# A new order for the first batch of a fused attention and mixture-of-experts kernel, with one half's q softmax moved to ScalarE and 24 identity turns on TensorE

## The chip, the cores and the metric

The kernel runs on one core of a Trainium2 chip. The metric is the device time of one execution in microseconds, the median of several runs. A core has a matmul engine (TensorE, "PE" in the profile, with its weight loads as "PEld"), a vector engine (VectorE, "DVE"), an engine for activation functions (ScalarE, "ACT"), a general engine (GpSimd, "POOL"), and queues that issue DMA transfers (here mostly "SP"). Each engine works through its own list of instructions in order. An instruction waits until the semaphores that it names are up, and all that stands behind it on its engine waits too.

## The reference

All data are float32. Three steps follow each other:

```python
# linear attention, 8 batches x 8 heads, 576 tokens, 64 channels
q_s = exp(q - max(q, -1));  q_s /= sum(q_s, -1) + 1e-9       # softmax over the channels
k_s = exp(k - max(k, 2));   k_s /= sum(k_s, 2) + 1e-9        # softmax over the tokens
kv  = einsum('bhsd,bhse->bhde', k_s, v)
x   = einsum('bhsd,bhde->bhse', q_s, kv)   # then laid out as (4608 tokens, 512)

# mixture of 8 experts, top 1: logits = x @ w_gate, e = argmax(logits)
out[token] = gate * sigmoid(x @ w_output_gate)[e] * (relu(x @ w1[e]) @ w2[e])

# second layer
h = max(max(x @ m_w1, x @ m_w2), x @ m_w3);  result = h @ m_wo
```

## The kernel before

Nearly all work is matmuls of the experts and of the second layer, which are run as three products of split operands. Ahead of them stands the attention of one batch and its routing, since the expert's weights to load are known only when the router has chosen. The kernel therefore runs in slots: slot 0 and later issue one group of 12 expert matmuls each (`l1_group`, `l2_group`), and the attention of the following batches, the splitting of weights and the routing are hung between the groups as events. Slots below 0 hold the first batch's attention with no expert work beside it. The list `first` gives its order: entry i becomes the event of slot i - 120. All engines' lists come from this one order, since the schedule is written by hand and nothing is moved afterwards.

A batch is worked in two units of four heads (the second argument 0 or 1), and a unit's result in two pairs (the third argument). The steps of a unit are:

- `load_k`, `load_q`, `load_v`: transfers issued on SP. `load_2` does the three for unit 0 of batch 1.
- `k_max` (DVE, tile `kmx`), `k_tr` (TensorE turns `kmx` into `kT`, DVE reduces it to `m` and makes the diagonal `dg`), `k_exp` (TensorE spreads `dg` as `kB`, DVE subtracts it from `k`, ACT takes the exponential into `ke`).
- `q_max` (DVE, `qm`), `q_exp` (subtraction on DVE, for unit 1 of batch 0 on POOL, then ACT's exponential in place), `q_sum` (DVE sum `qs`, + 1e-9, reciprocal), `q_norm` (DVE, `qn`).
- `kv_mm` (TensorE, 20 small matmuls), `kv_norm` (DVE, `kvraw`, and a transfer to memory).
- per pair: `q_tr` (five TensorE turns of `qn` into the PSUM tile of tag "big", one buffer, copied by ACT to `qTf`), `x_mm` (two matmuls of 288 columns into PSUM tiles of tag "mm", four buffers, which ACT copies to `xr`), the split of `xr` into a high part (ACT, `xs`) and a low part (`x_lo`, DVE, `xs`), and `logit_mm`.
- `logit_tr`, `route_1`, `route_2`: logits to tokens, the choice, counts, and the chosen expert's number, which SP reads to issue the loads of the first weights (`stg`). `route_3` makes the gates.
- `in_2` runs a step for unit 0 of batch 1. That unit's `k_tr` and `k_exp` come in slot 0 and the slots ahead of it (`EARLY`), with the split of the first weights (`w`, high part on ACT, low part on DVE for the first two).

The matmuls of the first expert group (`hp`) stand on TensorE behind that unit's `kB`.

Of the kernel before, what the change touches and what calls it, by code (L numbers as in the profile page):

```python
# [9 lines left out]
F32 = mybir.dt.float32  # L10
# [3 lines left out]
ACTF = mybir.ActivationFunctionType  # L14
ALU = mybir.AluOpType
AX = mybir.AxisListType
# [3 lines left out]
B, H, S, D = 8, 8, 576, 64  # L20
# [8 lines left out]
HF = S // 2  # L29
# [31 lines left out]
def tile_linear_attention__then__moe(  # L61
# [15 lines left out]
    nc = tc.nc  # L77
    dma = nc.sync.dma_start
    gdma = nc.gpsimd.dma_start
    vec = nc.vector  # L80
    act = nc.scalar.activation
    mm = nc.tensor.matmul
# [5 lines left out]
    ident = const.tile([128, 128], F32, name="ident")  # L88
# [35 lines left out]
    ps_mm = es_moe.enter_context(tc.tile_pool(name="ps_mm", bufs=4, space=PSUM))  # L124
# [5 lines left out]
    sm = es_att.enter_context(tc.tile_pool(name="sm", bufs=2, side="right"))  # L130
    dc_p = es_att.enter_context(tc.tile_pool(name="dc_p", bufs=1, side="right"))
    kvz = es_att.enter_context(tc.tile_pool(name="kvz", bufs=1, side="right"))
    ps_at = es_att.enter_context(tc.tile_pool(name="ps_at", bufs=1, space=PSUM, side="right"))
# [49 lines left out]
    units = {}  # L183
# [35 lines left out]
    def k_max(b, hb):  # L219
# [3 lines left out]
            out=u["mx"], in_=u["k"].rearrange("p h c d -> p h d c"), axis=AX.X, op=ALU.max  # L223
        )

    def q_max(b, hb):
        u = units[b, hb]
        qt = u["q"].rearrange("p h c d -> p (h c) d")
        m = sm.tile([128, 20, 1], F32, tag="qm", name="qm")
        vec.tensor_reduce(out=m[:, :, 0], in_=qt, axis=AX.X, op=ALU.max)  # L230
        u["qm"] = m

    def q_exp(b, hb):
        u = units[b, hb]
        qt = u["q"].rearrange("p h c d -> p (h c) d")
        eng = nc.gpsimd if (b, hb) == (0, 1) else vec
        eng.tensor_tensor(out=qt, in0=qt, in1=u["qm"].to_broadcast([128, 20, D]), op=ALU.subtract)
        act(out=qt, in_=qt, func=ACTF.Exp)

    def k_tr(b, hb):  # L240
        u = units[b, hb]
        ps = ps_at.tile([128, 2, 128], F32, tag="kb", name="kT")
        mx = u["mx"].rearrange("p h d -> p (h d)")
        for i in range(2):
            nc.tensor.transpose(ps[:, i], mx[:, 128 * i:128 * i + 128], ident)
        m2 = sm.tile([128, 2], F32, tag="m2", name="m2")
        vec.tensor_reduce(out=m2, in_=ps, axis=AX.X, op=ALU.max)
        u["dg"] = sm.tile([128, 2, 128], F32, tag="dg", name="dg")
        for i in range(2):
            vec.tensor_scalar(  # L250
                out=u["dg"][:, i], in0=ident, scalar1=m2[:, i:i + 1], scalar2=None, op0=ALU.mult
            )
# [93 lines left out]
    def x_mm(b, hb, pr):  # L346
        u = units[b, hb]
        g = 2 * hb + pr
        if b == 0:
            ps = [ps_mm.tile([128, HF], F32, tag="mm", name="xT0") for i in range(2)]  # L350
        else:
            big = ps_at.tile([128, 2, 512], F32, tag="big", name="xT")
            ps = [big[:, i, 0:HF] for i in range(2)]
        qT = u["qT", pr]
        for i in range(2):
            cs = slice(HF * i, HF * i + HF)
            if b < NFULL:
                mm(ps[i], kvraw[hb][:, pr], qT[:, 0, cs], start=True, stop=True)
                continue
            kv = u["kv"]  # L360
            for n, (a, c) in enumerate(((0, 0), (0, 1), (1, 0))):
                mm(ps[i], kv[:, a, pr], qT[:, c, cs], start=(n == 0), stop=(n == 2))
        xr = u["xr", pr] = xr_p.tile([128, S], F32, tag="xr", name="xr")
        if b == 0:
            for i in range(2):
                act(out=xr[:, HF * i:HF * i + HF], in_=ps[i], func=ACTF.Copy)
            if hb == 1:
                return
        else:
            act(out=xr.rearrange("p (a t) -> p a t", a=2), in_=big[:, :, 0:HF], func=ACTF.Copy)  # L370
        t = xp[b, g] = (x_po if b % 2 else x_pe).tile([128, 2, S], F32R, tag="x", name="xs")
        act(out=t[:, 0], in_=xr, func=ACTF.Copy)

    def x_lo(b, hb, pr):
        xr = units[b, hb]["xr", pr]
        if b == 0 and hb == 1:
            t = xp[b, 2 * hb + pr] = (x_po if b % 2 else x_pe).tile([128, 2, S], F32R, tag="x", name="xs")
            act(out=t[:, 0], in_=xr, func=ACTF.Copy)
        t = xp[b, 2 * hb + pr]
        vec.tensor_tensor(out=t[:, 1], in0=xr, in1=t[:, 0].bitcast(F32), op=ALU.subtract)  # L380
# [131 lines left out]
    def in_2(b, f):  # L512
        f(1, 0)

    first = (
        (load_k, 0), (load_k, 1), (load_q, 0), (load_v, 0), (load_q, 1), (load_v, 1),
        (k_max, 0), (k_tr, 0), (k_max, 1), (k_exp, 0), (k_tr, 1), (q_max, 0), (k_exp, 1), (q_exp, 0),
        (kv_mm, 0), (q_max, 1), (q_sum, 0), (kv_mm, 1), (q_norm, 0), (q_exp, 1), (kv_norm, 0), (q_tr, 0, 0), (kv_lo, 0),
        (load_2,), (q_sum, 1), (q_lo, 0, 0), (q_tr, 0, 1), (x_mm, 0, 0), (kv_norm, 1), (q_lo, 0, 1), (kv_lo, 1),
        (q_norm, 1), (q_tr, 1, 0), (x_mm, 0, 1), (logit_mm, 0, 0), (q_tr, 1, 1), (x_mm, 1, 0), (logit_mm, 0, 1),  # L520
        (x_mm, 1, 1), (x_lo, 0, 0), (x_lo, 0, 1), (logit_mm, 1, 0), (logit_mm, 1, 1), (in_2, q_max), (in_2, k_max),
        (logit_tr,), (route_1,), (route_2,), (in_2, q_exp), (x_lo, 1, 0), (x_lo, 1, 1), (route_3,),
    )
    for i, (f, *a) in enumerate(first):
        at(-120 + i, f, 0, *a)
    at(ROUTE0[0], route_4, 0)
    for c in range(5):
        at(ROUTE0[1] + 2 * c, route_5, 0, c)
    START = {n: 16 * n - 51 for n in range(2, 2 * B)}
    FRONT = (q_max, q_exp, k_max, k_tr, k_exp, q_sum, kv_mm, kv_norm, kv_lo, q_norm)  # L530
    BACK = (q_tr, q_lo, x_mm, x_lo, logit_mm)
    for n, s0 in START.items():
        b, hb = divmod(n, 2)
# [345 lines left out]
    with tc.manual_schedule():  # L879
# [55 lines left out]
        def out_ps(nm):  # L935
            return ps_o.tile([128, 512], F32, tag="o", name=nm)
# [401 lines left out]
        for c in range(6):  # L1338
# [41 lines left out]
            for i, (col, x) in enumerate(tiles):  # L1380
                m = CAP if x is None else 128
                if i < 2:
                    ps = o[i]
                else:
                    ps = out_ps("op")
# [16 lines left out]
    with tc.For_i(0, n_trip, 1) as it:  # L1402
# [9 lines left out]
        ps = out_ps("lqT")  # L1412
# [9 lines left out]
        for i in range(4):  # L1422
            ps = out_ps("lm")
# [11 lines left out]
        for f in range(6):  # L1435
# [15 lines left out]
            h = lp.tile([128, 2, SLOT], F32R, tag=f"lh{f}", name="lh")  # L1451
# [3 lines left out]
        ps = out_ps("lo")  # L1455
# [40 lines left out]
```

## Time and profile before

| | us |
|---|---|
| median of 3 runs | 1206.53 |
| lowest, highest | 1205.19, 1210.18 |
| the profiled execution, its own time | 1209.64 |
| its span, first to last instruction | 1207.9 |
| TensorE busy in the span | 1146.5 (95%) |
| VectorE busy | 799.1 (66%) |
| ScalarE busy | 527.4 (44%) |
| GpSimd busy | 411.2 (34%) |

The profiled execution lay 1.69 us outside its span, and 3.11 us above the median of the runs. Busy shares are averages over the whole span; the stretch that the change touches is the first 51 us, and it is read from the order of instructions there.

### The profile page before, as it was taken

How to read it: one execution, taken by the hardware profiler on the slowest of the kernel's cores; microseconds unless marked ns; L12 is line 12 of the kernel's file. 1: busy time of each engine (PE TensorE's matmuls, PEld its weight loads, DVE VectorE, ACT ScalarE, POOL GpSimd, SP SyncE). 2: the span in 40 equal slices, each digit the busy share in tenths (PEclk: the TensorE clock that was granted, in tenths of full speed). 3: DMA queues.
4: the chain of work that ended last, by engine and by line, in shares of the span. 5: the costliest groups of instructions: out<-in, count | busy, mean ns of one | idle time of the engine just before them, and what ended most of it. 6: DMA issues, size and time to landing. Idle time of an engine off the chain costs nothing. (4 is left out here: it accounts for less than half of the span.)

```text
span 1207.9 us, 21422 instructions
## 1 busy us (share of the span) xinstructions
PE 1146.5 (95%) x7626; PEld 1072.1 (89%) x7626; DVE 799.1 (66%) x1500; ACT 527.4 (44%) x1081; POOL 411.2 (34%) x502
## 2 busy tenths in 40 slices
PE   4699999999989999999999999999999999999994
PEld 3599898989989898999999899899899989989983
DVE  7688788787878879655789565555546545564430
ACT  2454454635545453545455433443344244333220
POOL 1156667677666767768342030000000000000000
PEclk9899899999999999999999999999999999999997
DMA  6785557575645764436599588397768848747701
GB/s 162 181 224 135 160 170 218 153 208 156 180 159 170 203 177 137 137 115 204 195 311 311 176 256 285 134 296 242 235 217 272 270 144 286 242 149 221 225 26 41
DMA packets 204207, 234.95 MB, mean 195 GB/s; under 512 B 78253, under 2 KB 122061, under 8 KB 204096
## 3 DMA queue, kind: packets, MB, share of 16 engines
q1 hardware_dynamic: 202384, 233.14, 62.4%
q8 instruction: 62, 1.02, 0.3%
q0 software_dynamic: 1712, 0.39, 0.2%
q14 instruction: 49, 0.40, 0.1%
HBM read 189.56 MB, written 44.13 MB: 193 GB/s over the span
## 5 line engine op out<-in xcount | busy, mean ns | idle before, releaser
L638 PE MATMUL yp<-h,w 128*128 128x288 f32 x1536 | 227.0, 304 | 0.0
L620 PE MATMUL hp<-xs,w 128*128 128x288 f32 x1536 | 218.6, 299 | 0.0
L638 PEld LDWEIGHTS yp<-h,w 128*128 128x128 f32 x1536 | 213.1, 192 | 3.3
L620 PEld LDWEIGHTS hp<-xs,w 128*128 128x128 f32 x1536 | 208.2, 189 | 2.6
L604 POOL TENSOR_TENSOR w<-stg,w 128x512 fp32r<-128x512 f32 x126 | 181.2, 1441 | 68.5 <-ACT w L597 66.7
L1218 PE MATMUL pY<-t,sw 128*128 128x384 f32 (+1 forms) x972 | 193.5, 342 | 1.3 <-ACT s L1227 0.9
L1218 PEld LDWEIGHTS pY<-t,sw 128*128 128x128 f32 x972 | 172.8, 188 | 5.5 <-ACT s L1227 2.1
L1195 POOL DMA_INDIRECT out_dram<-ocx,ftb x1 | 1.0, 981 | 481.7 <-SPq L1402 481.7
L1306 PE MATMUL op<-wo,hc 128*128 128x512 f32 (+1 forms) x666 | 156.2, 394 | 0.0
L1306 PEld LDWEIGHTS op<-wo,hc 128*128 128x128 f32 (+1 forms) x666 | 125.1, 188 | 27.9
L1227 ACT ACTIVATE s<-pY 128x384 f32<-128x384 f32 (+1 forms) x108 | 53.7, 497 | 133.1 <-PE pY L1218 129.2
L626 DVE SCALAR_TENSOR_TENSOR h<-hp,h 128x288 fp32r<-128x288 f32 x128 | 56.6, 451 | 54.8 <-ACT h L625 54.4
L625 ACT ACTIVATE h<-hp 128x288 fp32r<-128x288 f32 x128 | 52.3, 409 | 83.1 <-PE hp L620 82.6
L597 ACT ACTIVATE w<-stg 128x512 fp32r<-128x512 f32 x128 | 78.9, 620 | 0.0
L1218 PE MATMUL pY<-B,sw 128*128 128x384 f32 (+1 forms) x324 | 66.4, 340 | 0.5 <-DVE y L645 0.5
L1218 PE MATMUL pZ<-B,sw 128*128 128x384 f32 (+1 forms) x324 | 66.8, 341 | 0.1
L1218 PE MATMUL pX<-B,sw 128*128 128x384 f32 (+1 forms) x324 | 66.9, 341 | 0.0
L1218 PE MATMUL pX<-t,sw 128*128 128x384 f32 (+1 forms) x324 | 66.5, 340 | 0.0
L1234 ACT ACTIVATE hc<-c 128x384 fp32r<-128x384 f32 (+1 forms) x72 | 38.2, 531 | 61.4 <-DVE c L1257 61.1
L1218 PEld LDWEIGHTS pZ<-B,sw 128*128 128x128 f32 x324 | 58.0, 188 | 2.2 <-DVE c L1251 0.4
L1218 PEld LDWEIGHTS pX<-B,sw 128*128 128x128 f32 x324 | 57.7, 188 | 1.7
L1218 PEld LDWEIGHTS pY<-B,sw 128*128 128x128 f32 x324 | 57.7, 188 | 1.7 <-DVE y L645 0.8
(246 smaller groups left out, 1764.0 us busy)
## 6 DMA issues: line engine op xcount, KB each, us to landing
sw<-ws_d SPq DMA_DIRECT2D x315, 256.0 KB, 3.5
stg<-in_moe_w_dram SPq DMA_DIRECT2D x31, 1024.0 KB, 5.3
ws_d<-sw SPq DMA_DIRECT2D x63, 256.0 KB, 3.4
fw<-in_moe_w_dram SPq DMA_DIRECT2D x48, 256.0 KB, 4.1
v<-in_v_dram SPq DMA_DIRECT2D x80, 128.0 KB, 4.7
draw<-in_moe_w_dram SPq DMA_DIRECT2D x24, 384.0 KB, 4.0
k<-in_k_dram SPq DMA_DIRECT2D x16, 512.0 KB, 5.3
q<-in_q_dram SPq DMA_DIRECT2D x16, 512.0 KB, 6.9
```

The source lines that it names most:

```text
L597: act(out=t[:, 0], in_=src, func=ACTF.Copy)
L604: eng.tensor_tensor(out=t[:, 1], in0=src, in1=t[:, 0].bitcast(F32), op=ALU.subtract)
L620: mm(ps, w[:, a, kk], xp[b, kk][:, c, cs], start=(n == 0), stop=(n == 11))
L625: act(out=h[:, 0, cs], in_=ps, func=ACTF.Relu)
L626: vec.scalar_tensor_tensor(out=h[:, 1, cs], in0=ps, scalar=0.0, in1=h[:, 0, cs].bitcast(F32), op0=ALU.max, op1=ALU.subtract,)
L638: mm(ps, w[:, a, f], ht[f][:, c, cs], start=(n == 0), stop=(n == 11))
L1195: nc.gpsimd.indirect_dma_start(out=out[:, :], out_offset=bass.IndirectOffsetOnAxis(ap=tb[0:n, 0:1], axis=0), in_=src, in_offset=None, boun ...
L1218: mm(ps[:, 0:nn], w[:, a, kap], tt_[key, kap][:, cc, 0:nn], start=(start and k == 0), stop=(k == 5), skip_group_check=True)
L1227: act(out=t[:, 0:n_of(c)], in_=pst[n, "X" if nm == "sx" else "Y"][:, 0:n_of(c)], func=ACTF.Copy)
L1234: act(out=h[:, 0, cols], in_=t[:, 0:nn], func=ACTF.Copy)
L1306: mm(ps[0:m], hc[f][:, a, col:col + m], wo[f][:, cc], start=(f == F_ORDER[0] and i == 0), stop=(f == F_ORDER[5] and i == 2))
```

## The change

It touches the first batch only, and within it:

- Unit 0's q. `q_neg` takes the negated maximum on DVE. `q_rows` then issues 20 small ACT instructions of 128x64, one for each (head, chunk), which take exp(q - max) with the maximum as a bias of each partition and give the row's sum in the same instruction (5 of them ahead of unit 0's `ke`, 15 behind it). DVE's subtraction and its sum over `q` for unit 0 are gone; `q_inv` keeps the + 1e-9 and the reciprocal.
- `spin` issues 24 turns of the identity into the PSUM tile "big". Nothing reads the result.
- Unit 1's `kT` goes to a PSUM tile of tag "mm" in place of "kb".
- Of unit 1, the second half of each `xr` is copied by DVE in place of ACT. The high part of `xs` for unit 0 is now made in `x_lo`, as it was for unit 1.
- The list `first` has another order; the diff has it whole.

```diff
+    def q_neg(b, hb):
+        u = units[b, hb]
+        qt = u["q"].rearrange("p h c d -> p (h c) d")
+        m = u["qm"] = sm.tile([128, 20, 1], F32, tag="qm", name="qm")
+        vec.tensor_reduce(out=m[:, :, 0], in_=qt, axis=AX.X, op=ALU.max, negate=True)
+        u["qs"] = sm.tile([128, 20, 1], F32, tag="qs", name="qs")
+
+    def q_rows(b, hb, i0, i1):
+        u = units[b, hb]
+        qt = u["q"].rearrange("p h c d -> p (h c) d")
+        for i in range(i0, i1):
+            act(out=qt[:, i], in_=qt[:, i], func=ACTF.Exp, bias=u["qm"][:, i], accum_out=u["qs"][:, i])
+
+    def q_inv(b, hb):
+        s = units[b, hb]["qs"]
+        vec.tensor_scalar(out=s, in0=s, scalar1=1e-9, scalar2=None, op0=ALU.add)
+        vec.reciprocal(out=s, in_=s)
+
+    def spin(b, n):
+        ps = ps_at.tile([128, 1024], F32, tag="big", name="spin")
+        for i in range(n):
+            nc.tensor.transpose(ps[:, 0:128], ident, ident)
...
-    def q_exp(b, hb):
+    def q_exp(b, hb, parts=(0, 1)):
...
+        if 0 in parts:
+            eng.tensor_tensor(out=qt, in0=qt, in1=u["qm"].to_broadcast([128, 20, D]), op=ALU.subtract)
+        if 1 in parts:
+            act(out=qt, in_=qt, func=ACTF.Exp)
...
+        if (b, hb) == (0, 1):
+            ps = ps_mm.tile([128, HF], F32, tag="mm", name="kT0")[:, 0:256].rearrange("p (i d) -> p i d", i=2)
+        else:
+            ps = ps_at.tile([128, 2, 128], F32, tag="kb", name="kT")
...
         if b == 0:
             for i in range(2):
-                act(out=xr[:, HF * i:HF * i + HF], in_=ps[i], func=ACTF.Copy)
-            if hb == 1:
-                return
+                if i == 1 and hb == 1:
+                    vec.tensor_copy(xr[:, HF:S], ps[1])
+                else:
+                    act(out=xr[:, HF * i:HF * i + HF], in_=ps[i], func=ACTF.Copy)
+            return
...
-        if b == 0 and hb == 1:
+        if b == 0:
...
     first = (
         (load_k, 0), (load_k, 1), (load_q, 0), (load_v, 0), (load_q, 1), (load_v, 1),
-        (k_max, 0), (k_tr, 0), (k_max, 1), (k_exp, 0), (k_tr, 1), (q_max, 0), (k_exp, 1), (q_exp, 0),
-        (kv_mm, 0), (q_max, 1), (q_sum, 0), (kv_mm, 1), (q_norm, 0), (q_exp, 1), (kv_norm, 0), (q_tr, 0, 0), (kv_lo, 0),
-        (load_2,), (q_sum, 1), (q_lo, 0, 0), (q_tr, 0, 1), (x_mm, 0, 0), (kv_norm, 1), (q_lo, 0, 1), (kv_lo, 1),
-        (q_norm, 1), (q_tr, 1, 0), (x_mm, 0, 1), (logit_mm, 0, 0), (q_tr, 1, 1), (x_mm, 1, 0), (logit_mm, 0, 1),
-        (x_mm, 1, 1), (x_lo, 0, 0), (x_lo, 0, 1), (logit_mm, 1, 0), (logit_mm, 1, 1), (in_2, q_max), (in_2, k_max),
-        (logit_tr,), (route_1,), (route_2,), (in_2, q_exp), (x_lo, 1, 0), (x_lo, 1, 1), (route_3,),
+        (k_max, 0), (k_tr, 0), (q_neg, 0), (q_rows, 0, 0, 5), (k_exp, 0), (q_rows, 0, 5, 20), (k_max, 1),
+        (k_tr, 1), (q_max, 1), (q_exp, 1, (0,)), (k_exp, 1), (kv_mm, 0), (spin, 24), (q_inv, 0), (q_norm, 0), (q_tr, 0, 0),
+        (q_exp, 1, (1,)), (kv_norm, 0), (kv_mm, 1), (q_tr, 0, 1), (load_2,), (q_sum, 1), (x_mm, 0, 0), (q_norm, 1),
+        (x_mm, 0, 1), (kv_norm, 1), (logit_mm, 0, 0), (q_tr, 1, 0), (logit_mm, 0, 1), (in_2, q_max),
+        (x_lo, 0, 0), (q_tr, 1, 1), (x_mm, 1, 0), (x_lo, 0, 1), (x_mm, 1, 1), (logit_mm, 1, 0), (logit_mm, 1, 1),
+        (logit_tr,), (route_1,), (route_2,), (in_2, k_max), (in_2, q_exp), (x_lo, 1, 0), (x_lo, 1, 1), (route_3,),
     )
```

On TensorE, from unit 1's turn of `kmx` to the first product of `x`, the kernel before has (`kv_305` is unit 0's small product, `kv_332` unit 1's; line numbers are those of each kernel's file):

```order
L245 MATMUL kT<-ident,kmx 128x128 x2
L257 MATMUL kB<-dg,ones 128x256
L295 MATMUL kv_305<-v_199,ke 64x65 x20
L295 MATMUL kv_332<-v_200,ke 64x65 x20
L329 MATMUL qT<-ident,qn 128x128 x4
L330 MATMUL qT<-ident,qn 128x64
L329 MATMUL qT<-ident,qn 128x128 x4
L330 MATMUL qT<-ident,qn 128x64
L358 MATMUL xT_394<-qTf,kvraw_202 128x288
```

and the changed kernel, from the same turn (`kv_327` is unit 0's, `kv_392` unit 1's):

```order
L275 MATMUL kT_311<-ident,kmx 128x128 x2
L287 MATMUL kB<-dg,ones 128x256
L325 MATMUL kv_327<-v_199,ke 64x65 x20
L249 MATMUL spin<-ident 128x128 x24
L359 MATMUL qT<-ident,qn 128x128 x4
L360 MATMUL qT<-ident,qn 128x64
L325 MATMUL kv_392<-v_200,ke 64x65 x20
L359 MATMUL qT<-ident,qn 128x128 x4
L360 MATMUL qT<-ident,qn 128x64
L388 MATMUL xT_436<-qTf,kvraw_202 128x288
```

The 24 identity turns stand where unit 1's product stood, and that product has moved behind the first pair's turns.

On VectorE, behind the choice of the expert (`mi` is its number, `nm` the last row of `route_2`; `k`, `q`, `kmx` and `qm` are now those of batch 1), the kernel before has:

```order
L437 TENSOR_SCALAR mi<-mc 128x1
L441 COPY cs<-cnt 128x80
L443 TENSOR_SCALAR nm<-v_502,mc 128x8
L237 TENSOR_TENSOR q<-q,qm 128x1280
L380 TENSOR_TENSOR xs<-xr,xs 128x576 x2
L453 TENSOR_TENSOR rz<-roh,rl 128x40
```

and the changed kernel:

```order
L469 TENSOR_SCALAR mi<-mc 128x1
L473 COPY cs<-cnt 128x80
L475 TENSOR_SCALAR nm<-v_542,mc 128x8
L222 TENSOR_REDUCE kmx<-k 128x256
L263 TENSOR_TENSOR q<-q,qm 128x1280
L412 TENSOR_TENSOR xs<-xr,xs 128x576 x2
L485 TENSOR_TENSOR rz<-roh,rl 128x40
```

The maximum over batch 1's `k`, which stood ahead of the logits' turn, now stands between the routing and the subtraction.

## Rows read from the trace of the kernel before

**Rows 1.** Windows: busy us and instructions of each engine, granted clock, DMA
```profile
core 0: us, PE busy (x) PEld busy (x) DVE busy (x) ACT busy (x) POOL busy (x), PEclk, DMA share, GB/s
0.00:51.21 51.21, 24.97 (x176) 16.57 (x177) 36.67 (x77) 18.02 (x29) 5.99 (x22) 0.93 0.64 151
51.21:1207.90 1156.69, 1121.53 (x7452) 1055.58 (x7450) 762.44 (x1423) 509.41 (x1052) 405.19 (x480) 0.98 0.63 196
```

**Rows 2.** Timeline of TensorE: start, us, operation, count [idle before <-releaser]
```profile
15.07 1.19 PE L257 MATMUL kB<-dg,ones 128*128 128x256 f32 x2 [1.12 <-DVE dg L250]
16.20 6.02 PE L295 MATMUL kv<-v,ke 128*64 128x65 f32 x80
24.93 1.12 PE L329 MATMUL qT<-ident,qn 128*128 128x128 f32 x4 [2.71 <-DVE qn L277]
...
31.81 2.11 PE L358 MATMUL xT<-qTf,kvraw 128*128 128x288 f32 x4
...
34.29 0.66 PE L329 MATMUL qT<-ident,qn 128*128 128x128 f32 x4
...
35.09 1.24 PE L358 MATMUL xT<-qTf,kvraw 128*128 128x288 f32 x4
...
37.87 0.98 PE L390 MATMUL lgT<-xr,wgt 128*32 128x128 f32 x20
...
50.58 1.19 PE L257 MATMUL kB<-dg,ones 128*128 128x256 f32 x2 [8.03 <-DVE dg L250]
51.21 3.25 PE L620 MATMUL hp<-xs,w 128*128 128x288 f32 x12
54.66 1.83 PE L295 MATMUL kv<-v,ke 128*64 128x65 f32 x40 [0.20 <-ACT ke L262]
```

**Rows 3.** Waits of TensorE from 51.2 us on: total us, times, longest
```profile
PE xT L362 <- DVE qTs L344: 14.3, 6, 2.6
```

**Rows 4.** Windows around slow stretches of TensorE, columns as in the first group
```profile
50.60:54.10 3.50, 3.50 (x13) 3.32 (x14) 2.72 (x4) 0.77 (x1) 0.00 (x0) 0.50 1.00 351
...
123.70:126.40 2.70, 0.06 (x2) 0.03 (x1) 2.70 (x4) 1.08 (x1) 1.85 (x3) 0.88 0.55 185
126.40:132.60 6.20, 6.20 (x24) 5.95 (x25) 3.76 (x7) 3.84 (x6) 3.87 (x4) 0.50 0.41 110
```

**Rows 5.** Timeline of VectorE, same columns
```profile
9.50 2.32 DVE L222 TENSOR_REDUCE kmx<-k 128x256 f32<-128x1280 f32 x1
...
22.05 0.99 DVE L269 TENSOR_SCALAR qs<-qs 128x20 f32<-128x20 f32 x1
...
23.39 1.49 DVE L277 TENSOR_TENSOR qn<-q,qs 128x1280 f32<-128x1280 f32 x1
...
37.18 2.37 DVE L222 TENSOR_REDUCE kmx<-k 128x256 f32<-128x1280 f32 x1
...
43.58 1.49 DVE L237 TENSOR_TENSOR q<-q,qm 128x1280 f32<-128x1280 f32 x1
46.97 1.43 DVE L380 TENSOR_TENSOR xs<-xr,xs 128x576 fp32r<-128x576 f32 x2 [1.91 <-ACT xs L378]
...
49.95 0.48 DVE L250 TENSOR_SCALAR dg<-ident,m 128x128 f32<-128x128 f32 x2
```

**Rows 6.** Timeline of ScalarE and of GpSimd, same columns
```profile
45.10 1.27 ACT L238 ACTIVATE q<-q 128x1280 f32<-128x1280 f32 x1 [4.84 <-DVE q L237]
...
20.68 2.33 POOL L237 TENSOR_TENSOR q<-q,qm 128x1280 f32<-128x1280 f32 x1 [15.88 <-DVE qm L230]
```

**Rows 7.** Unit 0's q, second transfer: its issue, then size and us to landing
```profile
3.51 1.23 SPq L196 DMA_DIRECT2D q<-in_q_dram  x1
...
q<-in_q_dram SPq DMA_DIRECT2D x1, 128.0 KB, 6.9
```

**Rows 8.** Groups of ScalarE instructions: count | busy us, mean ns | idle before
```profile
L1329 ACT ACTIVATE oc<-op,tsrc 128x512 f32<-128x512 f32 x32 | 22.0, 689 | 59.1 <-PE op L1306 45.7 <-issue 13.4
L1129 ACT ACTIVATE fraw<-fm 128x512 f32<-128x512 f32 x9 | 5.4, 598 | 4.7 <-PE fm L1108 4.7
L394 ACT ACTIVATE lgt<-lgT 32x64 f32<-32x64 f32 x8 | 1.6, 197 | 0.0
```

More of the change, by code (lines that the diff above doesn't have):

```diff
@@ L236, in q_exp @@
         eng = nc.gpsimd if (b, hb) == (0, 1) else vec
-        eng.tensor_tensor(out=qt, in0=qt, in1=u["qm"].to_broadcast([128, 20, D]), op=ALU.subtract)
-        act(out=qt, in_=qt, func=ACTF.Exp)
+        if 0 in parts:
+            eng.tensor_tensor(out=qt, in0=qt, in1=u["qm"].to_broadcast([128, 20, D]), op=ALU.subtract)
+        if 1 in parts:
+            act(out=qt, in_=qt, func=ACTF.Exp)
     def k_tr(b, hb):
         u = units[b, hb]
-        ps = ps_at.tile([128, 2, 128], F32, tag="kb", name="kT")
+        if (b, hb) == (0, 1):
+            ps = ps_mm.tile([128, HF], F32, tag="mm", name="kT0")[:, 0:256].rearrange("p (i d) -> p i d", i=2)
+        else:
+            ps = ps_at.tile([128, 2, 128], F32, tag="kb", name="kT")
         mx = u["mx"].rearrange("p h d -> p (h d)")
```

## Prediction

> **What bounds the kernel now.** I read the windows first. From 51.21 us to the end TensorE is busy 1121.5 of 1156.7 us; ahead of it, 25.0 of 51.2 [rows 1]. So the end is set by TensorE, by a stream that starts with the first expert group `hp` at 51.21 [rows 2], and its largest waits later (six, 14.3 us in all) are for VectorE inside the stream [rows 3]. What happens ahead of `hp` counts one to one: whatever moves its start moves the end. The sum is thus the start of `hp`.
>
> Second, TensorE's timeline, for what it waits for and at which clock. The clock column is no help ahead of the first change of level: it reads full speed from the start, yet `kB` takes 1.19 us at 15.07, the same as at 50.58, where the window shows 0.50 [rows 2, 4]. So until about 33 us the engine runs at the lower level, 1.2 GHz. At 24.93 four turns take 1.12 us and the pair of `x` at 31.81 takes 2.11; at 34.29 and 35.09 the same work takes 0.66 and 1.24, at 2.4 GHz [rows 2]. Unit 0's and unit 1's small products, 6.02 us without a break from 16.20, did not raise it; the mix of turns and `x` products around 31.81 did.
>
> Third, VectorE's timeline behind the choice of the expert: the subtraction at 43.58, ACT's exponential at 45.10, ACT's high parts, VectorE's low parts at 46.97 after 1.91 us of waiting for them, the gates, `dg` at 49.95, `kB` at 50.58, `hp` at 51.21 [rows 2, 5, 6]. This is a chain from 43.58 to 51.21, 7.6 us, in which each step waits for the one before.
>
> **The change part by part.**
>
> *To unit 0's small product.* Before, `kmx` of unit 1 started at 9.50, as soon as VectorE was free [rows 5]. Now `q_neg` stands there. It needs unit 0's q, whose second transfer was issued at 3.51 and took 6.9 us: 10.4 [rows 7]. VectorE idles 0.9 us, takes the maximum (1.5 by the row of the same 1280 elements, `qn` [rows 5]) to 11.9, subtracts from k (1.5) to 13.4, and starts unit 1's `kmx` (2.3) only there. So `kmx` ends at 15.65 in place of 11.82. From there to `kB` it was 3.25 us, of which the subtraction, now ahead, was 1.4: `kB` at 17.5 in place of 15.07 [rows 2], +2.4. Unit 0's product stands behind it on TensorE's list: 18.7 to 21.7 (half of 6.02 [rows 2]) in place of 16.2 to 19.2.
>
> *The rows on ACT.* Twenty instructions of 64 elements with a pointer as bias and a sum. Not in the trace. Below: the 64-element copy, 0.197 us. For the pointer: 0.689 against 0.598 us for 512 elements with and without one, +0.09 [rows 8]. That is 0.29. The sum's price shows in no row; I bound it by nothing and by as much again, so 0.2 (they overlap and the sum is free) to 0.6, and take 0.3, nearest to the rows. ACT starts at 11.9, does five (1.5), `ke` of unit 0 (1.3), fifteen (4.5): done at 19.2, at 0.6 at 25. The Trainium skill (ScalarE: Activation LUTs, What ACT_TABLE_LOAD costs) gives 280 ns plus 0.833 ns an element with a pointer and an overlap of 93 ns back to back, from which I estimate 0.24 us a row and an end at 18; no price of the sum is there.
>
> *q ready.* VectorE takes unit 1's q maximum (17.4 to 18.9), then its subtraction from k to 20.4. GpSimd's subtraction starts with that maximum, 18.95 to 21.3 (2.33 [rows 6]). Before, the + 1e-9 took 0.99 us at 22.05 and ended just when GpSimd did, at 23.01 to 23.04 [rows 5, 6]; the same stall now ends at 21.3. Reciprocal, `qn` (1.49): ready at 23.2, against 24.88 [rows 5]. The removed subtraction and sum (3 us) thus give 1.7, since the later `kmx` takes the rest.
>
> *The identity turns.* They start at 21.7 behind unit 0's product. Four turns start within 0.65 us at the low clock and 0.33 at the high one: by 1.12 and 0.66 less a last turn of some 0.45 and 0.3 [rows 2], about 0.215 and 0.11 each. 24 of them are 5.2 us low, 2.6 high. All low, they end at 26.9; high at once, at 24.3. Both are behind `qn` at 23.2, so the turns, not q, set the first `q_tr`. This is the cover of the rows on ACT too: up to about 0.5 us a row they cost nothing. The turns would raise the clock at some point if they count as the mix ahead of 33 us did, which held turns. I take a rise near the end of the spin: `q_tr` at 26.8 in place of 24.93, **+1.9**.
>
> *From there to the last logit.* Before: 24.93 to 38.85, 13.9 us, nearly 9 of it at the low clock. Now at the high one: four `q_tr` at 0.8 (34.29 to 35.09), unit 1's small product that came in here (1.83), four pairs of `x` at 1.24, four `lgT` at 0.49 [rows 2]: 3.2 + 1.8 + 5.0 + 2.0 = 12.0. Unit 1's exponential now stands on ACT behind the copy of the first `qT`, so its sum, reciprocal and `qn` end some 6.4 us after the first `q_tr`, just as TensorE has done the 6.4 us that stand ahead of unit 1's first turns: perhaps 0.5 of waits. 12.5 against 13.9, **-1.4**. The copies moved from ACT to VectorE and the later high parts lie beside this.
>
> *`k_max` of batch 1.* Before, its 2.37 us at 37.18 lay under the wait for the logits: free. Now it stands at the head of the 7.6 us chain, ahead of the subtraction, and nothing in that chain waits for anything but itself: **+2.4**. Loading the first weights starts from `mi`, ahead of it, and is done within the chain, so it covers nothing.
>
> Sum: 1.9 - 1.4 + 2.4 = **+2.9**: `hp` at about 54.1, the profiled execution at 1209.64 + 2.9 = 1212.5. That execution was 3.1 above the median of the runs, 1206.53, so for a median 1206.53 + 2.9 = **1209.4**.
>
> **The rivals.**
>
> *The turns don't raise the clock* (slower). The small products are short matmuls with a weight load each, as the turns are, and 6.02 us of them raised nothing [rows 2]. Then the spin ends at 26.9, unit 1's product takes 3.0, the turns some 1.4 a pair, and `x` starts at 32.5; the clock rises some 5 us into `x`, as before, at 36 to 39. The stretch takes 15.5 to 17.3 in place of 13.9. +2.0 + 1.6 to 3.4 + 2.4 = +6.0 to +7.8: 1212.5 to 1214.3. It decides if the first `q_tr` still runs low, that is if 24 turns count no more than the small products did. The Trainium skill (TensorE: Matmul & The Clock Gate, Part 4: PE-mode transpose) speaks for it: turns do not count as a busy engine the way matmuls do. The trace agrees only in part: turns were part of the work ahead of the rise near 33 us.
>
> *The later drops of the clock fall otherwise* (faster). In each batch TensorE waits some 2.4 us for VectorE; around the first such wait the clock fell, and the 6.2 us behind it ran at 0.50 [rows 4]. Half of 6.2 is 3.1 us for that one; a drop half as long would cost half of that, and there are six of the waits [rows 3]. Another start of the stream against the clock's own rhythm can lose two to four of these drops, or gain: 1209.4 - 4 to - 7, 1202 to 1205.5. For it: runs of the kernel before differ by 5 us. Against: the waits stay as long as they were.
>
> *The rows on ACT are dear.* At 0.8 us each, a third above my upper bound, q is ready at 31.3, the spin has long ended, and all that follows the first `q_tr` is 4.5 us later than forecast: 1214. Little speaks for it.
>
> **How the numbers follow.** Forecast (1207.5 to 1211.5) 0.55, turns without effect 0.24, drops otherwise or clock up early 0.17, dear rows 0.04. The range takes in most of the second and third: 1204.5 to 1214. Half a per cent, about what a measurement of this kernel tells from no change, is 6 us. Slower by more (above 1212.6) is most of the second and fourth case: 0.20. Faster by more (below 1200.5) needs nearly all drops gone: 0.04. Within: 0.76.
>
> **What would show it.** Right: `hp` at 53.5 to 55 in TensorE's timeline, `qT` starting right behind the last spin near 26.5 with turns at 0.11 us, `kmx` of batch 1 between `nm` and the subtraction, and the idle ahead of `kB` grown by over 2 us. Wrong: four turns of `qT` at 1.12 us behind the spin (the clock stayed down); `qT` waiting for `qn` after the spin (rows dearer than 0.5 us); `hp` ahead of 51.2, in which case the chain behind the routing wasn't the bound that I take it for.

## The result, and the profile after

The changed kernel is slower: 1217.99 us (median of 10 runs, 1213.72 to 1220.86) against 1210.04 for the kernel before beside it (10 runs, 1205.19 to 1211.91), ratio 1.0065 [1.0052, 1.0079]. Run once more beside other kernels it gave 1.0047 [1.0031, 1.0062]. The forecast was 1209.4 and "no change". Its profiled execution took 1213.72 us, span 1212.0.

Windows of the kernel after, split at its first `hp`; busy us and instructions of each engine, then granted clock, DMA share, GB/s; they answer [rows 1]:

```profile
0.00:53.02 53.02, 24.71 (x200) 17.99 (x201) 34.79 (x77) 22.21 (x66) 5.98 (x22) 0.89 0.64 161
53.02:1212.00 1158.98, 1120.27 (x7452) 1053.83 (x7450) 765.92 (x1423) 508.52 (x1052) 407.92 (x480) 0.98 0.62 195
```

`hp` starts 1.81 us later than before. But the stretch behind it, with the same 7452 matmuls, also takes 2.3 us longer (1158.98 for 1156.69), with TensorE busy 1.3 us less: it waits more. The profiled execution is the quickest of its ten runs; at the median there are some 4 us more, which one profile can't place.

TensorE's timeline after: start, us, operation, count [idle before and what ended it]; it answers [rows 2]:

```profile
17.65 1.19 PE L287 MATMUL kB<-dg,ones 128*128 128x256 f32 x2 [1.12 <-DVE dg L280]
18.77 3.02 PE L325 MATMUL kv<-v,ke 128*64 128x65 f32 x40
21.72 4.09 PE L249 MATMUL spin<-ident 128*128 128x128 f32 x24
25.87 0.66 PE L359 MATMUL qT<-ident,qn 128*128 128x128 f32 x4
...
37.83 0.52 PE L422 MATMUL lgT<-xr,wgt 128*32 128x128 f32 x10 [0.46 <-ACT xr L399]
...
45.60 0.69 PE L275 MATMUL kT<-ident,kmx 128*128 128x128 f32 x2 [3.64 <-DVE kmx L222]
52.39 1.19 PE L287 MATMUL kB<-dg,ones 128*128 128x256 f32 x2 [6.10 <-DVE dg L280]
53.02 3.44 PE L652 MATMUL hp<-xs,w 128*128 128x288 f32 x12
```

The turns run 21.72 to 25.8, and the four turns of `qT` right behind them take 0.66 us, not the 1.12 of [rows 2]: the clock is up. From there to the end of the last `lgT` it is 12.48 us. The waits ahead of `kT` and `kB` of batch 1 are those of the late `k_max`.

ScalarE's, VectorE's and GpSimd's timelines after, same columns; they answer [rows 5, 6]:

```profile
12.51 0.33 ACT L238 ACTIVATE q<-q,qm 128x64 f32<-128x64 f32 x1
12.74 0.19 ACT L238 ACTIVATION_READ_ACCUMULATOR q<-q,qm 128x1 f32 x1
12.84 0.33 ACT L238 ACTIVATE q<-q,qm 128x64 f32<-128x64 f32 x1
...
10.64 1.49 DVE L231 TENSOR_REDUCE qm<-q 128x20 f32<-128x1280 f32 x1 [1.10 <-DMA q<-in_q_dram]
...
20.28 1.06 DVE L242 TENSOR_SCALAR qs<-qs 128x20 f32<-128x20 f32 x1
...
18.98 2.33 POOL L263 TENSOR_TENSOR q<-q,qm 128x1280 f32<-128x1280 f32 x1 [14.19 <-DVE qm L255]
```

A row on ScalarE is two instructions, the second reading out the sum. The second starts 0.23 us behind the first, and the next row 0.10 behind that, so row follows row at 0.33 us (12.51 to 12.84).

TensorE's waits: us, times, longest. First those of the kernel after, over the whole execution (8.4 us of `kB` lie ahead of `hp`), then, from 60 us on, those of the kernel before with 24 turns added (e5 below):

```profile
PE xT L392 <- DVE qTs L374: 14.3, 6, 2.6
PE kB L287 <- DVE dg L280: 11.9, 8, 6.1
PE pY L1250 <- ACT s L1259: 2.5, 2, 1.6
...
PE hp L652 <- DVE h L658: 0.5, 1, 0.5
```
```profile
PE xT L367 <- DVE qTs L349: 14.2, 6, 2.6
PE kB L262 <- DVE dg L255: 3.6, 6, 1.0
PE hp L625 <- DVE h L631: 2.0, 1, 2.0
```

`xT` for `qTs` is as in [rows 3]. A wait of `hp` for `h`, near 577 us, is new: the profile of the kernel before has none.

### The profile page after: what moved, and what is told of

The parts are those of the page before. It is cut to its first block, busy times and chain, and to the rows that moved or that the text cites. A ratio compares the mean times of both kernels' runs of the same rounds, so it can differ in the third digit from the quotient of the medians.

```text
span 1212.0 us, 21511 instructions
## 1 busy us (share of the span) xinstructions
PE 1145.0 (94%) x7650; PEld 1071.8 (88%) x7650; DVE 800.7 (66%) x1500; ACT 530.7 (44%) x1118; POOL 413.9 (34%) x502
## 5 line engine op out<-in xcount | busy, mean ns | idle before, releaser
L657 ACT ACTIVATE h<-hp 128x288 fp32r<-128x288 f32 x128 | 52.2, 408 | 82.5 <-PE hp L652 82.1
```

What stands on the lines that cost most here:

```text
L657: act(out=h[:, 0, cs], in_=ps, func=ACTF.Relu)
```

## Experiments

Each ratio is to the kernel before, run on the same chip beside it. "Stretch" is the span less the start of the first `hp`, in one profiled execution. That start varies from execution to execution by up to about 1 us, and the executions of one kernel lie up to 9 us apart, so one stretch settles little; the ratios decide.

| run | ratio | first `hp` | stretch |
|---|---|---|---|
| kernel before | 1 | 51.21 | 1156.7 |
| e1 changed kernel again | 1.0047 [1.0031, 1.0062] | 53.32 | 1159.4 |
| e2 without the turns | 1.0018 [1.0000, 1.0036] | 54.01 | 1156.0 |
| e12 without the turns, again | 1.0027 [1.0014, 1.0039] | 54.26 | 1157.1 |
| e3 with `k_max` early | 1.0054 [1.0038, 1.0070] | 53.89 | 1161.3 |
| e8 with 12 turns | 1.0036 [1.0023, 1.0048] | 52.22 | 1158.5 |
| e6 with the turns late | 1.0052 [1.0034, 1.0070] | 53.20 | 1162.8 |
| e9 six long matmuls for the turns | 1.0075 [1.0056, 1.0095] | 56.98 | 1159.0 |
| e10 24 one-column matmuls for the turns | 1.0041 [1.0023, 1.0060] | 54.35 | 1160.8 |
| e11 96 of them | 1.0085 [1.0065, 1.0106] | 57.18 | 1160.9 |
| e17 turns, padded to 256 instructions | 1.0027 [1.0014, 1.0041] | 54.60 | 1162.4 |
| e4 before, `k_max` late | 1.0009 [0.9994, 1.0025] | 53.46 | 1156.0 |
| e5 before, 24 turns | 1.0028 [1.0013, 1.0044] | 51.19 | 1161.9 |
| e7 before, 36 turns late | 1.0028 [1.0014, 1.0041] | 50.97 | 1163.5 |
| e13 before, 24 one-column at the start | 1.0034 [1.0022, 1.0047] | 50.49 | 1163.8 |
| e14 before, 64 one-column at the start | 1.0007 [0.9996, 1.0018] | 50.02 | 1158.9 |
| e15 before, 20 turns at the start | 1.0050 [1.0036, 1.0063] | 50.27 | 1162.6 |
| e16 before, 24 one-column at the end | 1.0010 [1.0000, 1.0021] | 50.86 | 1159.2 |
| e18 before, 24 turns, padded to 256 | 0.9996 [0.9982, 1.0011] | 50.58 | 1159.7 |

### Which part costs (e1 to e4)

e1 is the changed kernel, unaltered.

> The changed kernel once more, unaltered, since its profiled execution (1213.72 us) was the fastest of ten runs around 1218. Theory A: the typical run is one in which the 24 identity turns do not raise the clock in time; a profile near 1218 then shows four turns of qT at 1.12 us behind the spin and hp starting at 56 to 58 us. Theory B: the spin raises the clock in every run, hp starts near 53 us, and the missing 4 us are lost later, at the low clock behind hp or in the batches.

e2 takes the turns out:

```diff
-(kv_mm, 0), (spin, 24), (q_inv, 0),
+(kv_mm, 0), (q_inv, 0),
```

> The changed kernel without the 24 identity turns; nothing that is computed is left out. Theory A (the turns usually run low and raise nothing): the first qT starts near 23.3 us in place of 25.9 to 26.9, the rest runs low as before, hp starts at 54 to 55.5 and the time is 2 to 4 us below the changed kernel. Theory B (the turns raise the clock): hp starts 1 to 2 us later than the 53.0 of the changed kernel's profile, and the time is 1 to 2 us above it.

e3 moves `k_max` of batch 1 back ahead of the last logits:

```diff
-(in_2, q_max), ... (route_2,), (in_2, k_max), (in_2, q_exp),
+(in_2, q_max), (in_2, k_max), ... (route_2,), (in_2, q_exp),
```

> The changed kernel with batch 1's k_max put back ahead of the logits' turn, behind q_max; nothing else. Theory A and B alike: the 7.7 us chain from the routing to hp loses 2.3 us, but on VectorE the 2.3 us now push the copies of xr that the last logits wait for by some 1.5 us, so that hp starts 0.8 us earlier, at about 52.2. If the whole 2.3 us are saved (hp at 50.7), the copies had slack that I don't see; if none, the move was free.

e4 does the opposite to the kernel before:

```diff
-(in_2, q_max), (in_2, k_max), (logit_tr,), (route_1,), (route_2,), (in_2, q_exp),
+(in_2, q_max), (logit_tr,), (route_1,), (route_2,), (in_2, k_max), (in_2, q_exp),
```

> The kernel before with one part of the change alone: batch 1's k_max moved behind route_2. If the 2.4 us of k_max stand on the chain to hp one to one, hp starts at 53.4 to 53.6 in place of 51.2 and the time is 2 to 2.5 us above the kernel before. If the chain has slack, under 1 us.

In e1 the four turns of `qT` behind the spin take 0.66 us again and `hp` starts at 53.32: the turns do raise the clock, and the loss lies behind `hp` (theory B). Without turns the first `hp` is later than with them (54.0 to 54.3 for 53.0 to 53.3), yet the kernel is quicker by 0.0020 to 0.0047, 2.4 to 5.7 us (e1 and e2, run beside each other, took 1216.29 and 1212.60). So neither theory of e2 holds whole: the turns help ahead of `hp`, by about 1 us, and lose more than 3 us behind it. e4 shows the price of the late `k_max`: 2.25 us at `hp`, and some 1 us at the end, where the interval takes in anything from nothing to 3. e3 shows that in the changed order the early place isn't free either: `hp` at 53.89, not at the 52.2 expected. TensorE's timeline of e3:

```profile
38.82 0.52 PE L422 MATMUL lgT<-xr,wgt 128*32 128x128 f32 x10 [1.33 <-ACT xr L399]
40.68 0.52 PE L422 MATMUL lgT<-xr,wgt 128*32 128x128 f32 x10 [1.35 <-ACT xr L399]
```

The last two logits now wait 1.3 us each, in the changed kernel 0 and 0.46. VectorE's and ScalarE's timelines of e3 show why:

```profile
35.23 2.37 DVE L222 TENSOR_REDUCE kmx<-k 128x256 f32<-128x1280 f32 x1
37.50 0.76 DVE L412 TENSOR_TENSOR xs<-xr,xs 128x576 fp32r<-128x576 f32 x1
...
38.35 0.41 ACT L399 ACTIVATE xr<-xT 128x288 f32<-128x288 f32 x1 [2.32 <-DVE xs L412]
```

VectorE's low part of unit 0's `x` (37.50) now stands behind `kmx`, and ScalarE's copy of unit 1's `x` needs the buffer that it reads.

### Do the turns cost by the start of hp, by their number, by their place? (e5 to e8)

e5 and e7 add turns to the kernel before; e6 and e8 alter those of the changed kernel:

```diff
 # e5, kernel before: behind unit 1's small product
-(kv_mm, 1), (q_norm, 0),
+(kv_mm, 1), (spin, 24), (q_norm, 0),
 # e6, changed kernel: from their place to the wait between routing and kB
-(kv_mm, 0), (spin, 24), (q_inv, 0), ... (x_lo, 1, 1), (route_3,),
+(kv_mm, 0), (q_inv, 0), ... (x_lo, 1, 1), (route_3,), (spin, 24),
 # e7, kernel before: in that wait
-(x_lo, 1, 1), (route_3,),
+(x_lo, 1, 1), (route_3,), (spin, 36),
 # e8, changed kernel
-(spin, 24)
+(spin, 12)
```

> The kernel before with one part of the change alone: the 24 identity turns behind both small products, in TensorE's 2.7 us of idle time there. The turns end near 26.5 us, so the first qT starts 1.6 us later, but all up to the logits runs at the high clock: hp between 50.3 and 51.5. Theory N (the turns cost only what they shift hp by): the time stays within 1 us of the kernel before. Theory S (runs with the turns lose some 3 us more to waits behind hp, as three profiles with them against three without suggest): 2.5 to 4 us above the kernel before.

> The changed kernel with the same 24 identity turns moved to TensorE's idle time between the routing and batch 1's kB, so that the number of instructions is the same as in the changed kernel. hp starts as without the turns, near 54.0. Theory N: the time is that of the kernel without turns (1212.6) or up to 2 us less, if the turns keep the clock up for hp (12 matmuls in 1.9 us in place of 3.3). Theory S in the form that the extra instructions themselves cost, wherever they are: near 1216 to 1217. Theory S in the form that the place counts: near 1212.

> The kernel before with 36 identity turns in the idle time between the routing and batch 1's kB, to bring hp up at the high clock. At the low clock they take 7.7 us of an idle time of 8, at the high one 4. If they raise the clock, hp starts at 51.2 as before, but its first 12 matmuls take 1.9 in place of 3.25 us and the time falls by 1 to 2 us. If the clock at hp's start is not worth that in the end, the time is that of the kernel before.

> The changed kernel with 12 identity turns in place of 24. They end at 24.3 in place of 25.9 to 26.4 us, still behind qn (23.1). If the clock has risen by then or rises in the small product behind them, hp starts 1 to 2 us earlier than with 24, at 51.5 to 52.5, and the time falls by as much, to about 1215.5; if it doesn't rise before the x products, hp starts at 54 to 55 and the time is near the 1212.6 of the kernel without turns only if the later loss goes with the early clock, else near 1217 to 1218.

e5 is the telling one. Its `hp` starts at 51.19, as in the kernel before, and expert group 240 at 569.78 against 569.73; it then loses 3.8 us at one place (the 1.3 more in the second layer are within what that layer takes from profile to profile, 611.9 to 616.9 us). TensorE's timeline there, first of the kernel before, then of e5:

```profile
569.73 12.88 PE L620 MATMUL hp<-xs,w 128*128 128x288 f32 x96
582.45 12.88 PE L638 MATMUL yp<-h,w 128*128 128x288 f32 x96
```
```profile
557.06 12.88 PE L643 MATMUL yp<-h,w 128*128 128x288 f32 x96
569.78 6.51 PE L625 MATMUL hp<-xs,w 128*128 128x288 f32 x48
578.31 8.15 PE L625 MATMUL hp<-xs,w 128*128 128x288 f32 x48 [2.01 <-DVE h L631]
```

Turns in the late wait (e6, e7) lose as much, and the gain that e7 was to bring did not come. e8's 12 turns raised the clock too (`hp` at 52.22) and lose as much behind `hp`. So neither the start of `hp` nor the time that the turns take explains the loss; it goes with their being there. The order of the instructions on the other four engines is the same, row for row, with the turns and without them.

### Number, or time and clock? (e9 to e12)

e9 to e11 replace the body of `spin` in the changed kernel; e12 is e2 again.

```diff
-nc.tensor.transpose(ps[:, 0:128], ident, ident)                # x24
+nc.tensor.matmul(ps[:, 0:512], lhsT=ident, rhs=<ident, 4 times>)  # e9, x6
+nc.tensor.matmul(ps[0:1, 0:1], lhsT=ident[:, 0:1], rhs=ident[:, 0:1])  # e10 x24, e11 x96
```

> The changed kernel, with the 24 identity turns replaced by 6 plain matmuls of the identity with four copies of itself (128x512): about the same TensorE time (24 x 0.17 us = 4.1 us) from a quarter of the instructions. Theory A (the loss behind the first expert matmul goes with the number of extra TensorE instructions): near the kernel without turns, ratio 1.0010 to 1.0030, stretch behind the first expert matmul 1156 to 1157.5 us. Theory B (it goes with TensorE's work and the raised clock ahead of that matmul): like the changed kernel, 1.0040 to 1.0065, stretch 1159 us or more. Under both the clock rises before the first q transpose (near 24 us).

> The changed kernel, with each of the 24 turns replaced by a matmul of one column by one column: the same number of instructions, hardly any TensorE work, so the clock should rise only near 33 us as it did without turns. Theory A (number of instructions): like the changed kernel, ratio 1.0040 to 1.0065, stretch behind the first expert matmul 1159 us or more. Theory B (TensorE's work and clock): like the kernel without turns, 1.0010 to 1.0030 and 1156 to 1157.5 us.

> As the run before with 96 one-column matmuls, the dose for theory A. Theory A: more than the 24 turns cost, ratio 1.007 or more (four times the 0.0035 between the kernel with and without turns would be 1.016). Theory B: up to the TensorE time that they take (96 matmuls of some 0.03 to 0.06 us, 3 to 6 us, in an idle time of 4.5 us): 1.0010 to 1.0045.

> The changed kernel without the turns once more, on the chip of the three runs beside it. If the turns carry the loss: ratio 1.0005 to 1.0030, stretch behind the first expert matmul near 1156 us. If the first reading of it was luck of the build or of the runs: 1.0040 or more.

e9 tells number and time not apart: each plain matmul was run in two passes, so that the six took 7.65 us, not 4.1, and held up the first `qT` until 29.61; it lost 9.1 us with `hp` 5.8 us late. A one-column matmul takes two passes as well, so e10 added 96 instructions and not the 48 of the turns. It ran low until 33 us, as without turns, and its ratio is higher than that of e12 beside it (1.0041 for 1.0027), but the intervals overlap: it speaks against theory B without settling it. e11's ratio lies where theory A has it, but 2.8 us of it are a later `hp` (the 96 filled 5.13 us). Behind `hp` its profile lost no more than e10's (1160.9 for 1160.8), and its ratio some 2.5 us more, for four times the instructions: little for a price per instruction. The next runs settle both.

### Extra instructions that cost no time (e13 to e16)

The kernel before, with one-column matmuls or turns ahead of everything, where TensorE waits until 7.94 us; in e16 behind its last output matmul.

```diff
-(k_max, 0), (k_tr, 0),
+(spin, 24), (k_max, 0), (k_tr, 0),     # e13, e14: one-column, 24 and 64; e15: 20 turns
```

> The kernel before, with 24 one-column matmuls (96 TensorE instructions, some 1.3 us) at the very start, where TensorE waits until 7.94 us anyway; the first expert matmul should stay near 51.2 us. Theory A (the shift of TensorE's instructions behind them costs): ratio 1.0020 to 1.0040, stretch behind the first expert matmul 1159 us or more. Theory B (the loss needs TensorE's time or clock in the prologue's last 30 us): 0.9985 to 1.0015, stretch near 1157 us.

> As the run before with 64 of them (256 instructions, some 3.4 us, still inside TensorE's first idle time). Theory A: loss again, 1.0020 to 1.0040; were it to vanish while 24 lose, it would go with the place in a block of code and not with the number. Theory B: 0.9985 to 1.0015.

> The kernel before, with 20 identity turns (40 instructions, 5 to 6 us at 0.27 us each) at the very start, in the same idle time; if they raise the clock there, the first rise is recorded well ahead of 33 us and the prologue may gain up to 2 us. Theory A: 1.0010 to 1.0040. Theory B: the clock falls back in the waits that follow, so 0.9970 to 1.0015.

> The kernel before, with the 24 one-column matmuls behind TensorE's last output matmul, where only the program's size changes and nothing stands behind them. Theory A (shift of what is behind) and theory B: 0.9985 to 1.0020. If the program's size or layout alone costs: 1.0020 to 1.0040.

TensorE's timeline of e13:

```profile
1.44 1.34 PE L229 MATMUL spin<-ident 128*1 128x1 f32 x48 [1.44 <-POOL ident masks.py:199]
7.91 0.69 PE L250 MATMUL kT<-ident,kmx 128*128 128x128 f32 x2 [5.14 <-DVE kmx L222]
```

24 matmuls of one column (96 instructions, two passes with a weight load each) are done 5 us before anything waits for TensorE, `hp` starts 0.7 us earlier than before, and the kernel loses 1.0034. With 256 instructions (e14) it loses nothing that can be told, 1.0007, and the two intervals don't overlap. At the end of the program (e16) 96 cost at most little, 1.0010. So extra instructions lose without any work or clock near `hp` (theory B falls), but not by their number (theory A's dose falls too): what matters is where the instructions behind them come to stand, and 256 brings that back. e15's 40 lose no less than the 96.

What repeats every 256? The queues' rows on the pages of the kernel before and the changed one (packets, MB, share of 16 engines):

```profile
q8 instruction: 62, 1.02, 0.3%
```
```profile
q8 instruction: 63, 1.03, 0.3%
```

In the records each q8 packet has 16,384 bytes, and one comes about every 128 matmuls with their 128 weight loads. I read it as TensorE's code, 64 bytes an instruction. Extra instructions move all later packets in the work. Counted from the start of expert group 224 (of 256, twelve matmuls each), the packets around it come at -10.7, +5.0 and +24.7 us in the kernel before and at -10.9, +5.2, +25.0 with 256 more (e14); with 48 more at -15.2, +2.2, +19.2 (the changed kernel) and -14.2, +2.4, +19.2 (e5); with 96 more at -18.3, -1.3, +16.5 (e13).

### Padding to 256 (e17, e18)

The changed kernel, and e5, each with 52 one-column matmuls (208 instructions) at the very start, to make 256 with the 48 of the turns:

```diff
-(k_max, 0), (k_tr, 0),
+(pad, 52), (k_max, 0), (k_tr, 0),     # pad: one-column matmuls, as in e10
```

> The changed kernel, turns and all, with 52 one-column matmuls (208 instructions, some 2.9 us) at the very start, where TensorE waits until 7.9 us; with the turns' 48 that makes 256 instructions more than without both. Theory F (the place of the 16,384-byte instruction transfers in the work decides): the transfers come back to where the kernels without extra instructions have them (near -11, +5 and +25 us from the start of the expert group number 224; the changed kernel has -15, +2 and +19), stretch behind the first expert matmul 1155.5 to 1157.5 us, hp near 53.2 as in the changed kernel, so ratio 1.0005 to 1.0030. Theory A (any extra TensorE instruction costs): 1.0045 to 1.0070.

> The kernel before with the 24 turns behind unit 1's kv products (e5: ratio 1.0028, stretch 1161.9 us) and the same 208 instructions at the very start. Theory F: the loss goes, ratio 0.9985 to 1.0015, stretch near 1157 us, no wait of hp for h near 577 us (2.0 us in e5). Theory A: 1.0025 to 1.0045 and the wait stays.

Both ratios came as theory F has them and below what theory A has. The q8 packets stand at -10.6, +5.1, +26.4 (e17) and -10.8, +4.8, +25.5 (e18). e18 against e5: 0.9996 for 1.0028, intervals apart. e17 against the changed kernel: 1.0027 for 1.0065 (apart) and 1.0047 (they overlap); it equals the kernel without turns (1.0018, 1.0027). e17's and e18's stretches missed (1162.4 and 1159.7, expected up to 1157.5): e17's profiled execution, 1218.75, was the longest of its twelve, 3.5 above their median. Its `hp` missed too, 54.60 for 53.2: unit 1's turn of `kmx` already started 0.9 us later than in e1 (16.75 for 15.84), and the turns took 4.95 us. TensorE's timeline of e18 at the place where e5 waited 2.01 us:

```profile
571.01 13.06 PE L630 MATMUL hp<-xs,w 128*128 128x288 f32 x96
583.91 12.88 PE L648 MATMUL yp<-h,w 128*128 128x288 f32 x96
```

No wait. What may carry it from the code's packets to TensorE shows in SP's queue. Between 562 and 566 us in e5, the row of q8 (packets, MB, share), and SP's timeline, which is the issue of transfers:

```profile
q8 instruction: 1, 0.02, 1.7%
```
```profile
562.95 0.47 SPq L761 DMA_DIRECT2D srb<-w_d  x1
563.46 1.61 SPq L762 DMA_DIRECT2D srb<-w_d  x1
565.11 0.47 SPq L761 DMA_DIRECT2D srb<-w_d  x1
```

and in e18, where no q8 packet falls there:

```profile
563.73 0.48 SPq L767 DMA_DIRECT2D srb<-w_d  x1
564.25 0.47 SPq L766 DMA_DIRECT2D srb<-w_d  x1
564.76 0.47 SPq L767 DMA_DIRECT2D srb<-w_d  x1
```

The issue that coincides with the packet takes 1.61 us instead of 0.47; the changed kernel has one of 1.46 at 564.47, with its packet. Over all twenty profiles, of SP's issues between 55 and 600 us that overlap a q8 packet 41 to 65% took over 0.9 us, of the others 11 to 14%. A long issue overlaps something more easily, but that is not it: by the packets that were under way 0.235 us behind an issue's start it is 38 to 71% against 11 to 15%. Behind it everything that SP still has to issue comes 1 us later, and the work on it slides along. In e5 VectorE's splits of the second layer's operands then fall beside GpSimd's work. VectorE's timeline of the kernel before, then VectorE's and GpSimd's of e5:

```profile
572.58 1.02 DVE L875 TENSOR_TENSOR B<-yr,B 128x384 fp32r<-128x384 f32 x2
573.52 1.85 DVE L782 TENSOR_TENSOR sw<-s,sw 128x256 fp32r<-128x256 f32 x2
575.30 0.45 DVE L626 SCALAR_TENSOR_TENSOR h<-hp,h 128x288 fp32r<-128x288 f32 x1
```
```profile
572.92 3.23 DVE L880 TENSOR_TENSOR B<-yr,B 128x384 fp32r<-128x384 f32 x2
576.06 1.82 DVE L787 TENSOR_TENSOR sw<-s,sw 128x256 fp32r<-128x256 f32 x2
577.81 0.45 DVE L631 SCALAR_TENSOR_TENSOR h<-hp,h 128x288 fp32r<-128x288 f32 x1
...
571.11 4.62 POOL L609 TENSOR_TENSOR w<-stg,w 128x512 fp32r<-128x512 f32 x3
```

The two `B` take 3.23 us (1.02 in the kernel before, 2.00 in e18), while GpSimd runs three splits of the first layer's weights from 571.11 to 575.7; `h` comes at 577.81 (575.30), and TensorE waits for it.

This wait sorts the twenty profiles. Eight kernels have TensorE's code where it stood or 256 further on (the kernel before, e2, e4, e12, e14, e16, e17, e18): seven have no wait of `hp` for `h` there, e12 has one of 0.7 us. Of the twelve others eleven have it, with 0.3 to 2.4 us, and only e10 has none. The times say the same: the loss by the ratio, less what the first `hp` came later, is -1.2 to +2.0 us in the seven of the eight that have a ratio, and 1.8 (e10) to 7.0 us in the twelve. In single profiles the two overlap more: from the first `hp` to the end of the experts 541.2 to 546.7 us against 544.1 to 549.1.

**Shown** is that the place of TensorE's code within blocks of 256 instructions decides some 2.4 to 4.6 us, as measured by adding and taking away instructions that do nothing. That the packets act by holding up SP's issues is **read from the trace, not tested alone**, and I have not followed each of the other waits (`kB`, the second layer's `pY` and `pZ`) to one packet. Why e15's 40 instructions lose as much as e13's 96 is open too.

No version beats the kernel before: e18, the quickest, is level with it.

## Why the prediction was wrong

By its own steps:

- **To unit 0's small product**: right. `kB` 17.65 (forecast 17.5), the product 18.77 to 21.8 (18.7 to 21.7).
- **The rows on ACT**: right. 0.33 us a row, within 0.2 to 0.6 and near the 0.3 taken; the last starts at 19.63. The sum is an instruction of its own, 0.19 us, of which 0.10 lengthen the step from row to row and the rest lies beside the next row. The Trainium skill (ScalarE: Activation LUTs, What ACT_TABLE_LOAD costs) gives 280 ns plus 0.833 ns an element with a pointer and an overlap of 93 ns, from which I estimated 0.24 us; the trace agrees, since a row takes 0.33 us and its sum starts 0.23 behind it, and what was missing is the sum's 0.10.
- **q ready**: right. `qn` 21.69 to 23.2 (23.2), the stall on + 1e-9 ends at 21.3 with GpSimd. Without turns `qT` starts at 23.85 (e12), so the turns do set the first `qT`, as said.
- **The turns**: mechanism right, size a little off. They raise the clock, though sooner than taken: 4.09 us in place of 5.1, `qT` at 25.87 in place of 26.8, so +0.9 and not +1.9 (4.58 us and 26.37 in e1). The first rival, that they don't raise it, fell: 24 turns, and nothing else, stand between the small product at 1.2 GHz and `qT` at 2.4. What spoke for it in the Trainium skill (TensorE: Matmul & The Clock Gate, Part 4: PE-mode transpose), that turns do not count as a busy engine the way matmuls do, does not agree with these traces.
- **To the last logit**: right, 12.48 us for 12.5.
- **`k_max` of batch 1**: right at `hp`, 2.31 us in the chain; 2.25 when it alone was moved (e4). The sign named for it came in another form: the idle time ahead of `kB` did not grow but fell from 8.03 to 6.10, since `kT` now stands in the same stretch with 3.64 of its own.
- **Sum**: `hp` at 53.0 to 53.3 for 54.1, +1.8 to +2.1 for +2.9.
- **"What happens ahead of `hp` counts one to one"**: here it failed. It holds in the kernels whose code behind stands where it stood: +2.8 and +3.05 at `hp` gave ratios of 1.0018 and 1.0027 (2.2 and 3.3 us, e2 and e12), with padding +3.4 gave 3.3 (e17) and -0.6 gave -0.5 (e18); e4 and e14 are off by 1 to 2 us (+2.25 gave 1.1, -1.2 gave +0.8). It fails as soon as TensorE's list is longer ahead of `hp` by something other than 256: e5 +0.0 at `hp` and 3.4 us (1.0028), e13 -0.7 and 4.1. The turns were costed by the TensorE time that they fill. Their 48 instructions shift the code of all 7452 matmuls behind, and this had no term. Measured, it is the 2.4 to 4.6 us between the padded and the unpadded changed kernel (1.0027 against 1.0047 and 1.0065), and 3.9 us in the other order (0.9996 against 1.0028).
- **The base**: the time forecast was built on 1206.53, the median of three runs. Ten runs beside the result, these three among them, gave 1210.04, more runs later 1210.2 to 1211.6. That is 3.5 us of the 8.6 by which 1209.4 was missed. The profiled execution, 1209.64, was nearer to the truth than the median that I preferred to it.
- **The rivals**: dear rows fell (0.33 us). "The drops of the clock fall otherwise" was the nearest: it says that the stretch behind `hp` isn't fixed. But it took only the clock as its cause, and its sign was wrong. Over all twenty profiles the stretch fits 1123.0 us plus 1.24 per us of TensorE's waits behind 60 us plus 0.29 per us at the low clock there, to within 1.2 us. Most of the excess of the changed kernel is waits: 22.3 us, and 23.4 in e1, against 20.3 in e2 and 21.2 in e12; its time at the low clock is hardly longer, 30.5 and 26.9 us against 30.0 and 24.9.

So of the loss of 5.7 to 7.9 us, about 2 are the later `hp`, for the 2.9 forecast. Padding takes away 2.4 to 4.6, by the place of TensorE's code. The 1.2 to 1.5 that are left are about what `hp` came later in e17's profile than without padding, and no more than the noise.

## What to carry to other kernels

Before an edit that adds instructions to an engine that runs to the end is credited or blamed for its timing, pad it: add do-nothing instructions in that engine's first idle time until the total shift is a whole code block (256 here), and measure again. A loss that vanishes is one of place, not of the idea. And take the base of a time forecast from as many runs as there are, the profiled one included.

## What was not expected of the hardware

- 24 matmuls of one column at the start, done 5 us before TensorE is needed, cost 4.1 us (1.0034) at the end of the program; 64 of them cost nothing that can be told (1.0007).
- An SP issue beside one of TensorE's 16,384-byte code packets took 1.46 and 1.61 us where its neighbours took 0.47. TensorE itself runs past most packets: groups of 96 matmuls took 12.88 us with one in them and without.
- 20 turns of the identity at 1.43 us raised the clock within the turns (20 in 3.77 us) and it fell back before the first product, so nothing was won. Windows of e15, columns as in [rows 4]:

```profile
4.30:7.70 3.40, 0.91 (x8) 1.00 1.00 286
8.00:24.00 16.00, 9.62 (x88) 0.50 0.77 148
```

- Late turns held the clock up longer, but not to `hp`: in e7 36 of them ran at the high level from 41.89 (4.13 us), and the granted clock stayed at 1.00 until 50.1 us (43.8 in the kernel before). It fell in the wait of 4.11 us behind them, and the first 12 `hp` took 3.10 us all the same, near the 3.25 of [rows 2].
- The small products, which raised nothing in the trace of the kernel before, ran at the high level once. In e13 the granted clock is 1.00 from 18.5 to 21.9 us, and unit 1's product takes 1.83 us in place of 3.0:

```profile
16.20 2.79 PE L300 MATMUL kv<-v,ke 128*64 128x65 f32 x40
19.20 1.83 PE L300 MATMUL kv<-v,ke 128*64 128x65 f32 x40 [0.21 <-issue]
```
